# Sparse attention and maxout layer on one core: k, q and x of batches 1 to 3 transposed by DMA

## The chip, the cores and the metric

The kernel runs on one core of a Trainium2 chip. What counts is the device time of one execution in microseconds (us). The kernel before was run twice: 197.19 and 196.74 us, median 196.97.

## What is computed

Four batches, eight heads, 768 tokens, 64 values a head. Each token attends to the tokens less than 16 away, and to 24 summaries, one for each block of 32 tokens: of k the maximum, of v the mean. The result goes, token by token with its heads side by side, through a maxout layer.

```python
k_sum = k.reshape(B, H, nb, block, D).max(axis=3)
v_sum = v.reshape(B, H, nb, block, D).mean(axis=3)
scores_l = scale * np.matmul(q, k.transpose(0, 1, 3, 2))
mask_l = np.abs(pos[:, None] - pos[None, :]) < window
scores_s = scale * np.einsum('bhsd,bhnd->bhsn', q, k_sum) + np.log(block)
scores_all = np.concatenate([np.where(mask_l, scores_l, -1e9), scores_s], axis=-1)
a = softmax(scores_all)
x = np.matmul(a, np.concatenate([v, v_sum], axis=2))     # then (3072, 512)
out = np.maximum(x @ w1, x @ w2) @ w_out
```

## The kernel before

**Attention** goes by batch `b` (0 to 3), head pair `hp` (0 to 3) and group `grp` (0 to 2, 256 tokens each). For every batch and head pair, `prep` does this for k and for q:

- The load (L280) brings 384 KB into `kqf`, one of six buffers. Each partition gets six tokens that follow one another in a head, so a row of memory is 6 x 64 floats, 1,536 B.
- A cast (L359) writes bf16 into `kqb`, one of four buffers, with the two heads of a token side by side.
- TensorE turns it (L378): six 128x128 transposes into one PSUM bank.
- For k, DVE copies the bank to `kx` in token order (L393). Then it takes the maximum over each block (L399, L403, L407), copies the keys for the odd windows (L414) and puts the summaries in place (L418).
- For q, ACT copies the bank to `qx` (L424), in two halves of 64 partitions, one for each head.

`scores` multiplies `kx` and `qx` (L450), takes the exponential on ACT (L462) and, for batches 1 to 3, multiplies with a mask of zeros and ones on DVE (L471, L477). For batch 0 the mask is added on TensorE (L439). `values` multiplies with `vx` (L496); DVE takes the reciprocal of the sums (L508) and scales the result into `xs` (L510). After every second head pair TensorE turns `xs` (L520) and DVE copies it to `xt` (L525), the input of the layer.

v is loaded into `vf` in rows of one token, 256 B (L318), cast into `vx` on POOL (L359), and its copies for the odd windows and its summaries are spread inside `vx`; in batches 1 to 3 by DMAs on SyncE (L304).

**Maxout** has one unit for each batch and group, twelve in all: four `hidden` steps of eight matmuls (L596) with a relu on ACT (L601), and two `out` steps (L610, L617), an ACT copy (L359) and a store (L628). It computes max(h1, h2) w_out as h1 w_out + relu(h2 - h1) w_out, with `w1o` = w1 w_out made once (L580).

**The order** is made when the kernel is built. `Plan.run` steps through a model of time: each operation has an engine, a duration in us and a priority, and an engine takes the first ready operation of its list. What comes out is one fixed order for each engine; on the chip every engine follows its own in order and waits where it must. For SyncE (SP) the planner books `ISSUE` = 0.55 us for each DMA, has at most `DEPTH` = 4 under way, and sends one after the other. All 92 DMAs of the kernel before are issued by SyncE.

Of the kernel before, what the change touches and what calls it, by code (L numbers as in the profile page):

```python
# [13 lines left out]
BF16 = mybir.dt.bfloat16  # L14
# [48 lines left out]
class Plan:  # L63
# [6 lines left out]
        self.tasks, self.port = [], 0.0  # L70

    def op(self, engine, us, fn, read=(), write=(), change=(), touch=(), behind=(), prio=0.0, label="",
           port=False):
        t = Task()
        t.port = port or engine == "POOL"
        t.engine, t.us, t.fn, t.label = engine, us, fn, label
        t.prio = (prio, len(self.tasks))
        t.new, t.behind = [*write, *change], behind
        t.deps = {w for b in (*read, *change) for w in b.writers}
        for b in t.new:  # L80
            b.writers.append(t)
        for b in (*read, *touch, *t.new):
            b.users.append(t)
        self.tasks.append(t)
        return t
# [16 lines left out]
    def run(self):  # L102
        waiting = {e: [] for e in self.LAG}
        for t in sorted(self.tasks, key=lambda t: t.prio):
            waiting[t.engine].append(t)
        busy = dict.fromkeys(self.LAG, 0.0)
        sent = [0.0] * self.DEPTH
        order, tick = [], 0
        while len(order) < len(self.tasks):
            now = tick * 0.02  # L110
            for e, queue in waiting.items():
                if busy[e] > now or (e == "SP" and sent[-self.DEPTH] > now):
                    continue
                t = next((t for t in queue if self.ready(t, now)), None)
                if t is None:
                    continue
                t.start = now
                if e == "SP":
                    busy[e] = now + self.ISSUE
                    t.done = max(sent[-1], now + 0.4) + t.us  # L120
                    sent.append(t.done)
                else:
                    busy[e] = t.done = now + t.us
                    if t.port:
                        self.port = t.done
                queue.remove(t)
                order.append(t)
            tick += 1
            assert now < 1000, [t.label for q in waiting.values() for t in q]
        for t in order:  # L130
            t.fn()
        return order
# [3 lines left out]
def kernel(  # L136
# [14 lines left out]
    nc = tc.nc  # L151
    B, H, S, D = 4, 8, 768, 64
# [6 lines left out]
    NM, J, VW = S // 128, S // 128, 66  # L159
    NEG = -29952.0  # L160
    plan = Plan()
    op = plan.op
# [4 lines left out]
    def tiles(name, n, shape, dt):  # L167
        return [const.tile(shape, dt, name=f"{name}{i}") for i in range(n)]
# [5 lines left out]
    def bank(buf, n=512, dt=F32):  # L174
        a = bank_tile[:, buf.slot]
        return (a if dt is F32 else a.bitcast(BF16))[:, 0:n]

    kqf = Ring(tiles("kqf", 6, [128, 2, J * D], F32))
    kqb = Ring(tiles("kqb", 4, [128, J, 2, D], BF16))
    kxr = Ring(tiles("kx", 4, [128, 2, NM, 128], BF16))  # L180
    qxr = Ring(tiles("qx", 4, [128, 2, S], BF16))
    pbr = Ring(tiles("pb", 12, [128, 4, 192], BF16))
    vfr = Ring(tiles("vf", 1, [128, H, NM, D], F32))
# [91 lines left out]
    kqin, kx, qx, xt = {}, {}, {}, {}  # L275

    def load_kq(b, hp, prio):
        for n, src in enumerate((k, q)):
            f = kqin[b, hp, n] = Buf(kqf)
            op("SP", 1.05, lambda f=f, src=src: nc.sync.dma_start(  # L280
                out=f.ap[:], in_=src[b, 2 * hp:2 * hp + 2].rearrange("h (p j) d -> p h (j d)", j=J)),
               write=[f], prio=prio, label=f"load {'kq'[n]}{b}{hp}")

# [71 lines left out]
    def copy(engine, n, aps, label, us=None, **kw):  # L355
# [4 lines left out]
             "POOL": nc.gpsimd.tensor_copy}[engine](out=o, in_=i)  # L360
        op(engine, us or 0.06 + n * RATE[engine], fn, label=label, **kw)

    def prep(b, hp, prio, k_on, q_on):
        kx[b, hp], qx[b, hp] = Buf(kxr), Buf(qxr)
        tag = f"{b}{hp}"
        pss = []
        for n, eng in enumerate((k_on, q_on)):
            f, src = kqin[b, hp, n], Buf(kqb)
            copy(eng, 768, lambda f=f, src=src: (
                src.ap[:].rearrange("p j h d -> p h j d"),  # L370
                f.ap[:].rearrange("p h (j d) -> p h j d", d=D)),
                 read=[f], write=[src], prio=prio, label=f"cast {'kq'[n]}{tag}")
            ps = Buf(banks, "kq")
            pss.append(ps)

            def turn(src=src, ps=ps):
                for j in range(J):
                    nc.tensor.transpose(out=bank(ps, S, BF16)[:, 128 * j:128 * j + 128],  # L378
                                        in_=src.ap[:, j].rearrange("p h d -> p (h d)"),
                                        identity=identity[:])  # L380

            op("PE", J * 0.056, turn, read=[src], write=[ps], prio=prio, label=f"turn {'kq'[n]}{tag}")
        kps, qps = pss

        def order(ps):
            return bank(ps, S, BF16).rearrange("p (j c) -> p c j", j=J)

        main, odd, ks = Buf(Ring([None])), Buf(Ring([None])), Buf(ksr)

        def even():  # L390
            return kx[b, hp].ap[:, 0].rearrange("p m c -> p (m c)")

        op("DVE", 0.96, lambda: nc.vector.tensor_copy(out=even(), in_=order(kps)),  # L393
           read=[kps], write=[kx[b, hp], main], prio=prio, label=f"place k{tag}")
        def fold(k):
            return half.ap[:, 0:nb * k].rearrange("p (n g) -> p n g", g=k)

        half, one, two = Buf(hfr), Buf(Ring([None])), Buf(Ring([None]))
        op("DVE", 0.28, lambda: (lambda e: nc.vector.tensor_tensor(  # L399
            out=fold(16), in0=e[:, :, 0:16], in1=e[:, :, 16:32], op=ALU.max))(  # L400
                even().rearrange("p (n g) -> p n g", g=block)),
           read=[main], write=[half, one], prio=prio, port=True, label=f"max k{tag}")
        op("DVE", 0.18, lambda: (lambda e: nc.vector.tensor_tensor(  # L403
            out=half.ap[:, 384:576].rearrange("p (n g) -> p n g", g=8), in0=e[:, :, 0:8], in1=e[:, :, 8:16],
            op=ALU.max))(fold(16)),
           read=[one], write=[half, two], prio=prio, port=True, label=f"max k{tag}")
        op("DVE", 0.27, lambda: nc.vector.tensor_reduce(  # L407
            out=ks.ap[:, 0:nb], in_=half.ap[:, 384:576].rearrange("p (n g) -> p n g", g=8), axis=AX.X,
            op=ALU.max),
           read=[two], touch=[half], write=[ks], prio=prio, port=True, label=f"max k{tag}")  # L410
        for us, at, n, to, frm in ((0.2, 64, 64, slice(0, NM), slice(0, NM)),
                                   (0.14, 0, 32, slice(0, NM - 1), slice(1, NM)),
                                   (0.1, 0, 32, slice(NM - 1, NM), slice(0, 1))):
            op("DVE", us, lambda at=at, n=n, to=to, frm=frm: nc.vector.tensor_copy(  # L414
                out=kx[b, hp].ap[:, 1, to, at:at + n], in_=kx[b, hp].ap[:, 0, frm, at:at + n]),
               read=[main], write=[kx[b, hp], odd], prio=prio, port=True, label=f"odd k{tag}")
        for e, at in ((0, 96), (1, 32)):
            op("DVE", 0.2, lambda e=e, at=at: nc.vector.tensor_copy(  # L418
                out=kx[b, hp].ap[:, e, :, at:at + 32],
                in_=ks.ap[:].rearrange("p (o n) -> p o n", o=1).to_broadcast([128, NM, 32])),  # L420
               read=[ks, odd], write=[kx[b, hp]], prio=prio, port=True, label=f"sums k{tag}")
        for a in range(2):
            r = slice(64 * a, 64 * a + 64)
            op("ACT", 0.8, lambda a=a, r=r: nc.scalar.copy(  # L424
                out=qx[b, hp].ap[r, a, :], in_=order(qps)[r]),
               read=[qps], write=[qx[b, hp]], prio=prio, label=f"place q{tag}")
# [59 lines left out]
    def values(b, hp, grp, pb, prio):  # L486
        ps, tag = Buf(banks, "av"), f"{b}{hp}{grp}"
# [17 lines left out]
        if hp == 0:  # L505
            xt[b, grp] = Buf(xtr)
        x, x_t = xs[b, grp], xt[b, grp]
        op("DVE", 0.18, lambda: nc.vector.reciprocal(out=inv.ap[:], in_=av()[:, :, :, D:D + 1]),  # L508
           read=[ps], write=[inv], prio=prio, label=f"inv {tag}")
        op("DVE", 0.42, lambda: nc.vector.tensor_tensor(  # L510
            out=x.ap[:, hp % 2], in0=av()[:, :, :, 0:D],
            in1=inv.ap[:].to_broadcast([128, 2, 2, D]), op=ALU.mult),
           read=[ps, inv], write=[x], prio=prio, label=f"x {tag}")
        if hp % 2 == 0:
            return
        xp = Buf(banks, "x")

        def turn():
# [7 lines left out]
            out=x_t.ap[:, hp - 1:hp + 1, :].rearrange("p h n -> p (h n)"),  # L526
            in_=bank(xp, 512, BF16)), read=[xp], write=[x_t], prio=prio, label=f"xt {tag}")
# [182 lines left out]
```

## Time and profile before

| | |
|---|---|
| median of the two runs | 196.97 us |
| the profiled execution | 197.19 us |
| its span in the profile | 195.5 us |
| TensorE busy | 169.6 us, 87% |
| DVE busy | 120.1 us, 61% |
| ACT busy | 115.9 us, 59% |
| DMA packets on SyncE's queue, share of 16 engines' span | 61.0% |
| SyncE waiting in front of stores (L628) for ACT | 71.3 us |

The span is the profiled stretch on the core; the time of the same execution is 1.7 us longer. TensorE's busy share is of matmuls whose ends are modelled, so a full TensorE isn't one at its peak. Busy shares are means over the whole span, and the stages differ: in the first 50 us TensorE is busy for 30.2 us, after 80 us all the time. The profile also shows the clock that TensorE was granted: full nearly everywhere, 0.50 between 28 and 40 us.

### The profile page before, as it was taken

What the parts mean: (1) busy time and instruction counts of PE and PEld (TensorE: products, weight loads), DVE (VectorE), ACT (ScalarE), POOL (GpSimd) and SP (SyncE); (2) the same over time, 40 slices, a digit from 0 to 9 for tenths busy, and PEclk for the clock granted to TensorE, in tenths of its full rate; (3) what the DMA queues carried; (4) which work ended last, traced back from release to release, by engine and by line L of the source; (5) the groups of instructions that cost most, each with busy time, mean ns of one, the idle gap of its engine ahead of it and who ended that gap; (6) DMA issues with size and microseconds to landing.
All of it is one profiled execution on the core that took longest, in us unless ns stands there. A gap on an engine that the chain in (4) does not pass through costs nothing.

```text
span 195.5 us, 4320 instructions
## 1 busy us (share of the span) xinstructions
PE 169.6 (87%) x1688; PEld 121.8 (62%) x1688; DVE 120.1 (61%) x377; ACT 115.9 (59%) x183; POOL 29.7 (15%) x44
## 2 busy tenths in 40 slices
PE   0278553699999979999999999999999999999991
PEld 0166443688856546776867858587786675665740
DVE  6529999999869496741998853459878640000000
ACT  8297692855893843432999947169875542443512
POOL 7820395423000041000500000000000000000000
PEclk9999975589999999999999999999999999999998
DMA  5999999999999979997598152032020110220203
GB/s 178 263 255 282 376 385 390 245 273 334 237 232 322 211 197 294 324 212 198 170 230 291 66 161 107 5 117 62 3 107 3 54 57 21 86 96 15 107 0 107
DMA packets 29972, 34.57 MB, mean 177 GB/s; under 512 B 7616, under 2 KB 25568, under 8 KB 29952
## 3 DMA queue, kind: packets, MB, share of 16 engines
q1 hardware_dynamic: 29952, 34.30, 61.0%
q8 instruction: 13, 0.21, 0.5%
q14 instruction: 7, 0.06, 0.1%
HBM read 25.17 MB, written 6.29 MB: 161 GB/s over the span
## 4 chain that ended last, share of the span: by engine, by line
PE 61%; DMA 2%; ACT 2%; DVE 1%; issue 0%; ACTq 0%
PE banks L617 19%; PE banks L596 18%; PE banks L610 10%; PE banks L496 4%; PE banks L450 3%; PE banks L378 3%; PE banks L520 2%; DMA vx<-vx 2%; PE banks L338 1%; ACT g L601 1%; ACT qx L424 1%; DVE kqb L359 0%; ACT o L359 0%; ACT pb L462 0%; DVE pb L471 0%
## 5 line engine op out<-in xcount | busy, mean ns | idle before, releaser
L596 PE MATMUL banks<-xt,wd 128*128 128x256 bf16 x384 | 47.5, 273 | 0.5 <-DVE xt L525 0.5
L617 PE MATMUL banks<-wo,g 128*128 128x512 bf16 x192 | 46.0, 379 | 0.0
L596 PEld LDWEIGHTS <-wd 128*128 128x128 bf16 x384 | 35.9, 98 | 5.5 <-issue 0.7
L601 ACT ACTIVATE g<-banks 128x512 bf16<-128x512 f32 x48 | 28.7, 597 | 15.1 <-PE banks L596 14.2
L462 ACT ACTIVATE pb<-banks 128x512 bf16<-128x512 f32 x48 | 26.9, 598 | 13.7 <-PE banks L450 13.5
L359 ACT COPY o<-banks 128x512 f32<-128x512 f32 x24 | 14.1, 587 | 30.8 <-PE banks L617 30.3
L617 PEld LDWEIGHTS <-g 128*128 128x128 bf16 x192 | 17.7, 98 | 18.2
L378 PE MATMUL banks<-identity,kqb 128*128 128x128 bf16 x192 | 17.2, 237 | 13.1 <-ACT kqb L359 8.4
L424 ACT COPY qx<-banks 64x768 bf16<-64x768 bf16 x32 | 25.3, 790 | 3.4 <-PE banks L378 2.9
L610 PE MATMUL banks<-w1o,xt 128*128 128x512 bf16 x96 | 23.6, 379 | 0.0
L378 PEld LDWEIGHTS <-kqb 128*128 128x128 bf16 x192 | 13.6, 106 | 15.5 <-ACT kqb L359 9.4
L450 PE MATMUL banks<-qx,kx 128*128 128x128 bf16 (+2 forms) x208 | 18.6, 228 | 4.3 <-DVE kx L418 4.1
L450 PEld LDWEIGHTS <-kx 128*128 128x128 bf16 x208 | 15.3, 105 | 9.3 <-DVE kx L418 5.3
L496 PE MATMUL banks<-vx,pb 128*128 128x65 bf16 x384 | 18.8, 196 | 1.2 <-DMA vx<-vx 1.2
L496 PEld LDWEIGHTS <-pb 128*128 128x128 bf16 x384 | 16.9, 100 | 4.7 <-issue 1.4
L359 ACT CAST kqb<-kqf 128x768 bf16<-128x768 f32 x16 | 13.1, 831 | 10.9 <-DMA kqf<-in_q_dram 8.8
L510 DVE TENSOR_TENSOR xs<-banks,inv 128x256 bf16<-128x256 f32 x48 | 18.9, 413 | 0.2
L393 DVE COPY kx<-banks 128x768 bf16<-128x768 bf16 x16 | 15.2, 948 | 2.5 <-PE banks L378 2.3
L508 DVE RECIPROCAL inv<-banks 128x4 f32<-128x4 f32 x48 | 8.3, 178 | 9.7 <-PE banks L496 9.1
L359 POOL CAST vx<-vf 128x1536 bf16<-128x1536 f32 x6 | 8.8, 1501 | 34.6 <-DMA vf<-in_v_dram 34.6
L343 DVE CAST vx<-banks 32x264 bf16<-32x264 f32 x16 | 6.9, 432 | 10.4 <-issue 5.3
L610 PEld LDWEIGHTS <-xt 128*128 128x128 bf16 x96 | 8.7, 98 | 7.2
(48 smaller groups left out, 174.9 us busy)
## 6 DMA issues: line engine op xcount, KB each, us to landing
kqf<-in_k_dram SPq DMA_DIRECT2D x16, 384.0 KB, 7.4
kqf<-in_q_dram SPq DMA_DIRECT2D x16, 384.0 KB, 7.1
out_dram<-o SPq DMA_DIRECT2D x20, 256.0 KB, 2.0
wf<-in_moe_w_dram SPq DMA_DIRECT2D x8, 512.0 KB, 8.1
wf<-in_moe_w_out_dram SPq DMA_DIRECT2D x4, 512.0 KB, 6.7
vf<-in_v_dram SPq DMA_DIRECT2D x2, 768.0 KB, 8.5
vx<-vx SPq DMA_DIRECT2D x9, 165.0 KB, 3.7
vx<-vx SPq DMA_DIRECT2D x3, 396.0 KB, 10.4
```

What stands on the lines that cost most here:

```text
L359: {"DVE": nc.vector.tensor_copy, "ACT": nc.scalar.copy, "POOL": nc.gpsimd.tensor_copy}[engine](out=o, in_=i)
L378: nc.tensor.transpose(out=bank(ps, S, BF16)[:, 128 * j:128 * j + 128], in_=src.ap[:, j].rearrange("p h d -> p (h d)"), identity=identity[:])
L393: op("DVE", 0.96, lambda: nc.vector.tensor_copy(out=even(), in_=order(kps)), read=[kps], write=[kx[b, hp], main], prio=prio, label=f"place ...
L424: op("ACT", 0.8, lambda a=a, r=r: nc.scalar.copy(out=qx[b, hp].ap[r, a, :], in_=order(qps)[r]), read=[qps], write=[qx[b, hp]], prio=prio, ...
L450: nc.tensor.matmul(out=o[:, :, n0:n1], lhsT=w, rhs=qx[b, hp].ap[:, :, c:c + n1 - n0], start=(mask_on != "PE"), stop=(mask_on != "PE" or (i ...
L462: op("ACT", 0.6, lambda: nc.scalar.activation(out=pv(), in_=bank(ps).rearrange("p (i w q) -> p i w q", w=2, q=64), func=ACT.Exp, scale=scale),
L496: nc.tensor.matmul(out=av()[:, u, a, :], lhsT=pb.ap[:, 2 * u + a, 64 * par:64 * par + 128], rhs=vx[b].ap[:, par, 2 * grp + u, 2 * hp + a, ...
L510: op("DVE", 0.42, lambda: nc.vector.tensor_tensor(out=x.ap[:, hp % 2], in0=av()[:, :, :, 0:D], in1=inv.ap[:].to_broadcast([128, 2, 2, D]), ...
L596: nc.tensor.matmul(out=bank(ps)[:, 256 * s:256 * s + 256], lhsT=wd[n].ap[:, c, 128 * s:128 * s + 128], rhs=x.ap[:, c, :], start=(c == 0), ...
L601: op("ACT", 0.6, lambda n=n, ps=ps: nc.scalar.activation(out=g.ap[:, 2 * n:2 * n + 2, :].rearrange("p f n -> p (f n)"), in_=bank(ps), func ...
L610: nc.tensor.matmul(out=bank(ps), lhsT=x.ap[:, c, sl], rhs=w1o[c].ap[:], start=(c == 0), stop=False)
L617: nc.tensor.matmul(out=bank(ps), lhsT=g.ap[:, f, sl], rhs=wo[f // 2].ap[:, f % 2, :], start=False, stop=(f == FC - 1))
```

## The change

It concerns batches 1 to 3; batch 0 stays as it was.

- k and q of these batches are loaded with one token to a row: partition p gets tokens p, 128 + p, 256 + p and so on, in 12 rows of 256 B.
- `flip` is a new step: a transposing DMA from SBUF to SBUF, issued by SyncE. For k it writes `kx` directly (128x768), for q a new tile `qt` (two buffers), for x it writes `xt` (128x512 for two head pairs).
- So the turns of k, q and x on TensorE (L378, L520), the copies of k and x on DVE (L393, L525) and that of q on ACT (L424) are left out for these batches. q goes from `qt` to `qx` by two copies on DVE.
- The planner books 1.2 us on SyncE and 0.7 us of transfer for a flip, and 1.75 us for a load in short rows.

```diff
     def op(self, engine, us, fn, read=(), write=(), change=(), touch=(), behind=(), prio=0.0, label="",
-           port=False):
+           port=False, issue=None):
         t = Task()
+        t.issue = issue or self.ISSUE
...
-                    busy[e] = now + self.ISSUE
+                    busy[e] = now + t.issue
                     t.done = max(sent[-1], now + 0.4) + t.us
...
+    qtr = Ring(tiles("qt", 2, [128, J, 128], BF16))
...
             f = kqin[b, hp, n] = Buf(kqf)
-            op("SP", 1.05, lambda f=f, src=src: nc.sync.dma_start(
+            op("SP", 1.75 if b else 1.05, lambda f=f, src=src: nc.sync.dma_start(
+                out=f.ap[:].rearrange("p h (j d) -> p (h j) d", d=D),
+                in_=src[b, 2 * hp:2 * hp + 2].rearrange("h (j p) d -> p (h j) d", j=J))
+               if b else nc.sync.dma_start(
                 out=f.ap[:], in_=src[b, 2 * hp:2 * hp + 2].rearrange("h (p j) d -> p h (j d)", j=J)),
...
+    def flip(src, to, write, prio, label):
+        def fn():
+            i, o = src.ap[:], to()
+            names = "p a b c -> p (a b c)" if len(i.shape) == 4 else "p a b c e -> p (a b c e)"
+            nc.sync.dma_start_transpose(out=o, in_=i.rearrange(names))
+        op("SP", 0.7, fn, read=[src], write=write, prio=prio, label=label, issue=1.2)
+
     def prep(b, hp, prio, k_on, q_on):
...
+            if b:
+                pss.append(src)
+                continue
             ps = Buf(banks, "kq")
...
-        op("DVE", 0.96, lambda: nc.vector.tensor_copy(out=even(), in_=order(kps)),
-           read=[kps], write=[kx[b, hp], main], prio=prio, label=f"place k{tag}")
+        if b:
+            flip(kps, lambda: kx[b, hp].ap[:, 0], [kx[b, hp], main], prio, f"flip k{tag}")
+        else:
+            op("DVE", 0.96, lambda: nc.vector.tensor_copy(out=even(), in_=order(kps)),
+               read=[kps], write=[kx[b, hp], main], prio=prio, label=f"place k{tag}")
...
+        if b:
+            qt = Buf(qtr)
+            flip(qps, lambda: qt.ap[:], [qt], prio, f"flip q{tag}")
         for a in range(2):
             r = slice(64 * a, 64 * a + 64)
+            if b:
+                op("DVE", 0.26, lambda a=a, r=r: nc.vector.tensor_copy(
+                    out=qx[b, hp].ap[r, a, :], in_=qt.ap[r].rearrange("p m c -> p (m c)")),
+                   read=[qt], write=[qx[b, hp]], prio=prio, port=True, label=f"place q{tag}")
+                continue
...
         if hp % 2 == 0:
+            return
+        if b:
+            flip(x, lambda: x_t.ap[:, hp - 1:hp + 1, :].rearrange("p h (u n) -> p (h u) n", u=2), [x_t], prio,
+                 f"flip x{tag}")
             return
         xp = Buf(banks, "x")
```

As durations and engines change, the planner makes a new order for every engine. SyncE's changed list holds 134 DMAs, in this sequence: loads of batch 0; twelve loads of weights, mixed with k, q and v of batch 1; the first flips of batch 1 with its spreads of v; then flips, stores of batch 0 and loads of batch 2 in turn; flips of x of batch 1, some of them behind the load and the spreads of v of batch 2. For batch 2 it is the same pattern: eight flips of k and q with stores of batch 1 and loads of batch 3 between them, then the flips of x, three of group 0 to 2 for the first two head pairs, two spreads of v of batch 3, and the flip of x for group 0. TensorE's changed list has, after the last values of batches 1 and 2, no step of an earlier batch's maxout left in front of the first unit of that batch.

## The prediction

> **What bounds the kernel now.** First the page's slices and its chain, to find the engine that sets the end; then the chain in order of time, to price that engine's work; then the stage windows, to see what runs at its limit beside it.
>
> ```profile
> PE   0278553699999979999999999999999999999991
> ...
> DMA  5999999999999979997598152032020110220203
> ...
> PE 61%; DMA 2%; ACT 2%; DVE 1%; issue 0%; ACTq 0%
> ```
>
> Each digit is a slice of 4.9 us. TensorE is full from 88 us (slice 19) to the end, and holds 61% of the chain. The DMA engines are full, with three small dips, from 5 to 108 us, and mostly idle from there. So there are two limits, one after the other, and the change adds to the second what it takes from the first.
>
> ```profile
> 93.19 1.75 PE banks L596 x16
> ...
> 111.09 0.45 PE banks L520 x8
> ...
> 129.54 0.67 PE banks L378 x12
> ...
> 165.21 3.49 PE banks L596 x32
> 168.71 1.73 PE banks L610 x8
> 170.43 3.45 PE banks L617 x16
> ...
> 191.31 0.58 ACT o L359
> ```
>
> Columns: start, length, work. One maxout unit (a batch and a group) is 3.49 + 1.73 + 3.45 = 8.67 us; a turn by TensorE costs 0.67/12 = 0.056 us for k and q and 0.45/8 = 0.056 us for x. The first unit of batch 1 starts at 93.19; 4.2 us lie between the start of the last copy out (191.31) and the end of the span.
>
> ```profile
> 38.00:40.00 2.00, 1.90 (x29) 1.75 (x27) 1.97 (x7) 1.95 (x3) 0.00 (x0) 0.50 1.11 218
> ...
> 96.00:98.00 2.00, 2.00 (x20) 1.49 (x18) 2.00 (x9) 1.98 (x4) 0.00 (x0) 1.00 0.72 149
> ...
> 102.00:104.00 2.00, 2.00 (x35) 1.65 (x34) 1.82 (x9) 1.96 (x4) 0.00 (x0) 1.00 1.06 384
> ```
>
> The last three figures are TensorE's clock, DMA share (a full queue reads 1.06 to 1.12) and GB/s. At 38 us v of batch 1 loads in rows of 256 B: 218 GB/s with full engines. At 102 us k and q of batch 3 load in rows of 1,536 B: 384 GB/s. At 96 us the spreads of vx run; between 96 and 102 us about 170 GB/s.
>
> [...]
>
> **The change part by part.**
>
> *TensorE.* Gone are 12 x 2 x 6 = 144 turns of k and q and 18 x 4 = 72 of x: 216 x 0.056 = 12.1 us, all in the stretch where TensorE is full. This is the gain if nothing else comes in its place.
>
> *ACT and DVE.*
>
> ```profile
> L424 ACT COPY qx<-banks 64x768 bf16<-64x768 bf16 x32 | 25.3, 790 | 3.4 <-PE banks L378 2.9
> L393 DVE COPY kx<-banks 128x768 bf16<-128x768 bf16 x16 | 15.2, 948 | 2.5 <-PE banks L378 2.3
> ...
> L525 DVE COPY xt<-banks 128x512 bf16<-128x512 bf16 x24 | 9.8, 420 | 4.5 <-PE banks L520 4.0
> ```
>
> ACT loses 24 x 0.790 = 19.0 us. DVE loses 12 x 0.948 + 18 x 0.420 = 18.9 us and gains 24 copies of q from SBUF; a copy of half their columns takes 0.257 us (L414), so 0.257 to 0.514 us each, I take 0.40: +9.6. Neither ended the chain after 88 us, and TensorE's work covers them, so I credit nothing. The new copies wait for a flip with later reciprocals behind them, and those free the banks of values: a late flip also holds the other head pairs' values back.
>
> *SyncE.* 42 transposing DMAs are added to 92. A plain issue takes about 0.45 us; no row shows a transposing one, and the planner books 1.2 us. Between the first flip and that of x (2, 0) SyncE issues 26 flips and 39 plain DMAs: 26 x 1.2 + 39 x 0.45 = 49 us in the 90 us or so that this stretch lasts. Covered by the transfers, unless an issue costs over 2.8 us. No gain is possible here.
>
> *The DMA engines.* A load of k or q is 393 KB: 1.02 us at 384 GB/s, 1.80 at 218. Over 24 loads, +18.7 us. A flip of k or q moves 197 KB, one of x 131 KB. [...]
>
> *What that does to the order.* In the changed order TensorE has the units of batch b-1 used up when it comes to batch b's: the values of batch 2 are followed by two sums and at once by unit (2, 0), which needs the last flip of x for group (2, 0). All queues are in order, so TensorE stands until it lands. Ahead of it on SyncE's queue lie, in DMA time: loads of batch 0, 8 x 1.02 + 7.2 for v; weights 12 x 1.34; together 31.5. Loads of k and q of batches 1, 2 and six of 3: 22 x 1.80 = 39.6. Three v: 3 x 7.2 = 21.6. Spreads, 0.95 MB a batch at 170 GB/s, twice, and the odd part of batch 3: 14.8. [...] Ten stores x 0.68 = 6.8. Sum 131.3 us.
>
> How near to that do they run? The same prices for the kernel before, up to v of batch 3 landing (issued 78.8, landed 92.5), give 24 x 1.02 + 28.8 + 16.1 + 9.2 + 3.4 = 82.0 us in 92.5 - 1.3 = 91.2: a pace of 0.90. So (2, 0) can start at 1.3 + 131.3/0.90 = 147.2 us. From there the rest is TensorE's: six units, 52.0; scores and values of batch 3, 4 x 0.68 + 12 x 0.243 = 5.6; the end, 4.2. Together 61.8, and **the span becomes 209 us**. The profiled execution took 197.19 for its span of 195.5, so +1.7: 210.7; the median of the runs is 0.2 lower. I say **210 us**.
>
> Does TensorE arrive earlier? The same count up to the flip of (1, 0) gives 92.2 us, so 1.3 + 92.2/0.90 = 103.7 for unit (1, 0) in place of 93.19; from there three units, attention 2 and its sums are 26.0 + 5.6 + 1.35 = 33.0: TensorE is ready at 136.7, and stands some 10 us twice.
>
> **The rivals.**
>
> *TensorE stays the bound* (faster). Span 195.5 - 12.1 = 183.4, so 185 us. For it: 61% of the chain, and after 110 us the DMA engines are mostly idle. Against: (2, 0) would have to start by 121.6, with 131.3 us of transfers ahead. [...] It ends faster than before from the point where (2, 0) starts before 195.5 - 61.8 = 133.7: at a pace of 0.90 that is 119 us of transfers, which leaves flips 4.9 us, too little for 4.5 MB; at a pace of 1.0, flips of 246 GB/s do. So this case needs gapless transfers.
>
> *Flips are dear.* [...] At 170 GB/s flips cost 26 us instead of 17: + 10 us, 221. [...] A cycle makes it worse: kqb is freed by a flip, the cast needs kqb, the load needs the cast's buffer, and the flip stands behind loads in the same queue.
>
> *The words say more than the diff.* Masks on VectorE (L471) and odd values by DMA (L304) are in the kernel before already; no time comes from them.
>
> *The clock falls.* At 30 to 40 us, where TensorE idled, the granted clock was 0.50. If two stops of 10 us bring that back for a few us each, some 3 us a stop; inside the range.
>
> **How the numbers follow.** [...] Dear flips or the cycle: 0.28, 216 and up. TensorE-bound or nearly: 0.17, 185 to 193. A difference of 2% (3.9 us) is about what can be told from no change: faster means below 193.0, slower above 200.9. Of the likeliest case 0.14 falls between these. So faster 0.17, same 0.14, slower 0.69. The range, 191 to 230, leaves out most of the TensorE-bound end and the worst of the dear flips.
>
> **What would show it.** Right: the DMA digits stay at 9 to about 145 us; unit (2, 0) starts near 147 with TensorE idle before it, released by a flip of xt; L378 falls to 48 instructions and L424 to 8; k and q loads run near 218 GB/s. Wrong: TensorE full from 90 us on (rival one), flips of over 1 us of DMA time each (rival two), or SyncE busy issuing flips with idle DMA engines, where I have called the issue covered.

## The result, and the profile after

| | before | after |
|---|---|---|
| median of two runs | 196.97 us | 217.41 us |
| the profiled execution | 197.19 us | 217.56 us |
| its span | 195.5 us | 215.8 us |
| TensorE busy | 169.6 us, 87% | 167.4 us, 78% |
| TensorE's granted clock, mean | 0.961 | 0.913 |
| DMA packets on SyncE's queue, share | 61.0% | 83.1% |
| DMA packets under 512 B | 7,616 | 73,472 |

The ratio after to before is 1.104, interval 1.0975 to 1.1101: slower by a tenth. In the experiments below a time is the median of all runs of a kernel, while its ratio leaves out runs more than 1.5% above that kernel's fastest, so the two can differ by about 1%. The page of the changed kernel, slices first (5.4 us each), then the chain by engine:

```profile
PE   1292855999978699280896999947939999999992
...
PEclk9999795699999999757699699996997999999999
DMA  5999999999998999999999999976978244202202
...
PE 42%; DMA 19%; SPq 15%; DVE 14%; issue 5%; ACT 3%; POOL 0%; ACTq 0%; DVEq 0%
```

The full stretch of the DMA engines, which ended at 108 us before, now reaches the end of slice 26, 140 us, and is followed by a 7 and a 6. TensorE has holes beside it, at 87 to 92 and 97 to 103 us (slices 17 and 19) and at 143 to 147 us (slices 27 and 28). TensorE's share of the chain falls from 61 to 42%. What takes its place is DMA (2% before), SyncE's own instructions (SPq, not listed before) and DVE (1% before).

TensorE's timeline, the stops of over 3 us after 90 us; the brackets hold the idle time ahead and what ended it:

```profile
91.97 1.48 PE L343 MATMUL banks<-vx,ones 128*128 128x264 bf16 x6 [4.51 <-POOL vx L364]
...
103.17 5.11 PE L627 MATMUL banks<-xt,wd 128*128 128x256 bf16 x30 [6.66 <-DMA xt<-xs]
...
147.19 5.10 PE L627 MATMUL banks<-xt,wd 128*128 128x256 bf16 x30 [4.22 <-DMA xt<-xs]
...
160.09 0.61 PE L477 MATMUL banks<-qx,kx 128*128 128x128 bf16 x8 [3.48 <-DVE qx L447]
```

The first line is the sums of v of batch 2, released by the cast of that v. The second and third are units (1, 0) and (2, 0), both released by a flip of x. They resume at 103.17 and 147.19 us; 103.7 and 147.2 were forecast. The last stop was not forecast: the scores of batch 3 wait for a late flip of q and its copy on DVE.

What released (2, 0), from the chain in order of time:

```profile
140.94 0.78 SPq L372
...
142.43 2.01 SPq L309
...
144.53 2.62 DMA xt<-xs
...
147.19 5.12 PE banks L627 x30
```

L372 is a flip, L309 a spread of v. The x that is turned here was ready at 140.9 (a DVE instruction that starts at 140.51 and takes 0.42); SyncE got past the two spreads ahead of it at 144.5 only, and the flip then took 2.62 us from issue to landing. So the last link is SyncE's time, not a full DMA queue (the slices there read 7 and 6).

Stage windows at 76 us (k and q in rows of 256 B) and behind the stop of (2, 0); the last three figures are clock, DMA share and GB/s:

```profile
76.00:78.00 2.00, 2.00 (x42) 1.91 (x39) 1.88 (x9) 1.57 (x3) 0.00 (x0) 1.00 1.33 223
...
148.00:150.00 2.00, 2.00 (x12) 1.39 (x11) 0.00 (x0) 0.60 (x1) 0.00 (x0) 0.50 0.67 148
```

The short rows run at 223 GB/s, near the 218 that v showed before (38 to 40 us). After the stop of 4.2 us the granted clock is 0.50.

### The profile page after: what moved, and what is told of

Same layout as the page of the kernel before. It is cut to its first block, busy times and chain, and to the rows that moved or that the text cites. A ratio compares the mean times of both kernels' runs of the same rounds, so it can differ in the third digit from the quotient of the medians.

```text
span 215.8 us, 3917 instructions
## 1 busy us (share of the span) xinstructions
PE 167.4 (78%) x1472; PEld 115.0 (53%) x1472; DVE 105.5 (49%) x371; ACT 98.2 (45%) x159; POOL 29.2 (14%) x44
## 2 busy tenths in 40 slices
DMA packets 89683, 41.63 MB, mean 193 GB/s; under 512 B 73472, under 2 KB 85280, under 8 KB 89664
## 3 DMA queue, kind: packets, MB, share of 16 engines
q1 hardware_dynamic: 89664, 41.38, 83.1%
## 4 chain that ended last, share of the span: by engine, by line
PE 42%; DMA 19%; SPq 15%; DVE 14%; issue 5%; ACT 3%; POOL 0%; ACTq 0%; DVEq 0%
PE banks L627 15%; PE banks L648 11%; SPq L282 7%; DMA xt<-xs 5%; PE banks L641 5%; SPq L372 4%; DMA qt<-kqb 4%; PE banks L523 4%; DMA kqf<-in_q_dram 3%; PE banks L477 3%; PE banks L611 3%; DMA wf<-in_moe_w_dram 3%; DMA kx<-kqb 2%; SPq L309 2%; DVE kx L437 2%
## 5 line engine op out<-in xcount | busy, mean ns | idle before, releaser
L627 PE MATMUL banks<-xt,wd 128*128 128x256 bf16 x384 | 53.4, 296 | 10.9 <-DMA xt<-xs 10.9
L627 PEld LDWEIGHTS <-wd 128*128 128x128 bf16 x384 | 39.5, 106 | 20.2 <-issue 11.6
L537 DVE TENSOR_TENSOR xs<-banks,inv 128x256 bf16<-128x256 f32 x48 | 19.3, 417 | 14.4 <-DMA xt<-xs 14.0
L523 PE MATMUL banks<-vx,pb 128*128 128x65 bf16 x384 | 20.8, 204 | 6.1 <-DVE pb L498 2.4
L523 PEld LDWEIGHTS <-pb 128*128 128x128 bf16 x384 | 18.5, 105 | 10.6 <-issue 4.3
L364 DVE CAST kqb<-kqf 128x768 bf16<-128x768 f32 x13 | 7.2, 564 | 25.0 <-DMA kx<-kqb 16.4
L393 PE MATMUL banks<-identity,kqb 128*128 128x128 bf16 x48 | 5.7, 285 | 11.0 <-ACT kqb L364 6.5
L343 PE MATMUL banks<-vx,ones 128*128 128x264 bf16 x48 | 8.6, 332 | 4.5 <-POOL vx L364 4.5
L573 POOL TENSOR_TENSOR wd<-wf,wf 128x1024 bf16<-128x1024 f32 x4 | 9.7, 2430 | 10.4 <-DVE xs L537 6.1
L393 PEld LDWEIGHTS <-kqb 128*128 128x128 bf16 x48 | 4.4, 131 | 11.8 <-ACT kqb L364 7.1
```

What stands on the lines that cost most here:

```text
L364: {"DVE": nc.vector.tensor_copy, "ACT": nc.scalar.copy, "POOL": nc.gpsimd.tensor_copy}[engine](out=o, in_=i)
L523: nc.tensor.matmul(out=av()[:, u, a, :], lhsT=pb.ap[:, 2 * u + a, 64 * par:64 * par + 128], rhs=vx[b].ap[:, par, 2 * grp + u, 2 * hp + a, ...
L537: op("DVE", 0.42, lambda: nc.vector.tensor_tensor(out=x.ap[:, hp % 2], in0=av()[:, :, :, 0:D], in1=inv.ap[:].to_broadcast([128, 2, 2, D]), ...
L573: op(wd_on, 2.1 if wd_on == "POOL" else 1.2, lambda: (nc.gpsimd if wd_on == "POOL" else nc.vector).tensor_tensor(out=wd[n].ap[:], in0=fs[1 ...
L627: nc.tensor.matmul(out=bank(ps)[:, 256 * s:256 * s + 256], lhsT=wd[n].ap[:, c, 128 * s:128 * s + 128], rhs=x.ap[:, c, :], start=(c == 0), ...
```

## The experiments

Two theories stand at the start. *Theory 1*, the prediction's: the volume of transfers ahead of the flips of x sets units (1, 0) and (2, 0). *Theory 2*: SyncE, which stands before stores and issues everything in order, sets them. *Theory 3* came up with the trace: the way of x itself (values, `xs`, issue and landing of a flip) leaves TensorE with nothing to do for 4 to 5 us at the end of batch 1 and of batch 2.

Each ratio is to the kernel before, run beside it on the same chip (its medians there: 195.5 to 196.3 us).

### Stores issued by ACT

```diff
-                nc.sync.dma_start(out=out[b * S + at:b * S + at + n, :], in_=o.ap[0:n])
+                nc.scalar.dma_start(out=out[b * S + at:b * S + at + n, :], in_=o.ap[0:n])
```

> The changed kernel with its 28 stores issued by ACT, right behind ACT's own copies, in place of SyncE; SyncE's order is else the same. Theory 1 (volume: the DMA engines' pace sets when unit (2, 0) can start): the volume is the same, so (2, 0) starts no earlier than 143 us (147.2 in the changed kernel), and the time is 213 to 219 us. Theory 2 (SyncE in order: flips stand behind stores that wait 36 us in all for ACT's copies): these waits go, (1, 0) starts 6 to 8 us earlier than 103, (2, 0) at 132 to 138, and the time is 201 to 208 us.

220.03 us, ratio 1.127 (1.120 to 1.133), 1 us above theory 1's numbers. SyncE's share of the chain falls from 15 to 5%. Unit (1, 0) resumes at 101.93 us, 1.2 us earlier, and unit (2, 0) does not move. TensorE's and SyncE's timeline of this kernel:

```profile
147.24 6.16 PE L627 MATMUL banks<-xt,wd 128*128 128x256 bf16 x30 [5.32 <-DMA xt<-xs]
```

```profile
79.86 7.37 SPq L282 DMA_DIRECT2D kqf<-in_k_dram  x1
...
140.08 1.18 SPq L309 DMA_DIRECT2D vx<-vx  x2
144.60 3.96 SPq L372 DMA_TRANSPOSE xt<-xs  x3
```

That (2, 0) stays where it was is not a clean result. SyncE is past the two spreads at 141.3, 3.2 us earlier than in the changed kernel, but issues the flip for (2, 0), the first of the three, at 144.60 only; in the changed kernel it follows the spreads at once (past them at 144.45, issued at 144.53). What takes the 3.3 us isn't shown. Without them (2, 0) would have come at about 143.9 (an estimate, 147.24 less 3.3), which is still 6 us behind the latest that theory 2 allowed. So waiting in front of stores explains at most some 3 us of (2, 0), and theory 2's numbers fall in this form.

The first line of the second fence shows something else that holds SyncE: the DMA right behind a load of v takes it 7.37 us although the trace names no wait for it. The changed kernel has the same behind its loads of v: a load of k at 42.03 us with 8.29, one at 125.25 with 7.45. What keeps SyncE there isn't shown.

### Rows of 1,536 B with the flips kept

```diff
-            op("SP", 1.75 if b else 1.05, lambda f=f, src=src: nc.sync.dma_start(
-                out=f.ap[:].rearrange("p h (j d) -> p (h j) d", d=D),
-                in_=src[b, 2 * hp:2 * hp + 2].rearrange("h (j p) d -> p (h j) d", j=J))
-               if b else nc.sync.dma_start(
+            op("SP", 1.75 if b else 1.05, lambda f=f, src=src: nc.sync.dma_start(
```

> The changed kernel with k and q of batches 1 to 3 loaded in rows of 1,536 B again, the planner's figures and so all orders unchanged. The flips then put the tokens in another order, so this leaves out the right order of tokens in kx and qx; the work is the same. Theory 1 (volume): 22 loads up to (2, 0) cost 0.78 us less each, 17 us of transfers, 19 us at the pace of 0.90; (2, 0) would start at the time when TensorE is ready, 134 to 138, and the time is 200 to 208 us. Theory 2 (SyncE in order, and its issue of 1.25 us a flip): little changes, 212 to 217 us.

205.48 us, ratio 1.041 (1.032 to 1.049). This kernel leaves out the right order of tokens in `kx` and `qx`; the order of all instructions is that of the changed kernel. Unit (2, 0) comes 12.4 us earlier:

```profile
134.79 4.76 PE L624 MATMUL banks<-xt,wd 128*128 128x256 bf16 x30 [3.76 <-DMA xt<-xs]
```

Theory 1's 134 to 138 and its time hold, and the rows alone are worth 0.063 of the time before. By volume, the 22 short-row loads ahead of that unit would give 22 x 0.78/0.90 = 19.1 us; two thirds of it are seen, so the rest of the way there isn't volume alone.

### The short rows alone, in the kernel before

Only the load is changed, and the copies take the turned tile as it comes, since it is in token order then.

```diff
+                out=f.ap[:].rearrange("p h (j d) -> p (h j) d", d=D),
+                in_=src[b, 2 * hp:2 * hp + 2].rearrange("h (j p) d -> p (h j) d", j=J))
+               if b else nc.sync.dma_start(
...
+            if b:
+                return bank(ps, S, BF16)
```

> The kernel before with one part of the change alone: k and q of batches 1 to 3 loaded in rows of 256 B (turned on TensorE and placed in token order as before; the planner's figures unchanged). Theory 1 (volume): 114.3 us of transfers ahead of (2, 0) at a pace of 0.90 are done at 128, just when TensorE wants it (130.2), and 84.2 ahead of (1, 0) at 95, 2 us late: 197 to 199 us. Theory 2: no SyncE waits are added, 196.5 to 198. A third: short rows alone are most of the loss (they hold up the head pairs one after the other): over 205 us.

205.69 us, ratio 1.048 (1.042 to 1.054). Theory 1's number missed, and so did theory 2's; what was listed third, over 205 us, is what came. TensorE's timeline, before and with short rows, at the end of its wait for the last spread of vx of batch 1:

```profile
72.38 0.49 PE L496 MATMUL banks<-vx,pb 128*128 128x65 bf16 x11 [0.72 <-DMA vx<-vx]
```

```profile
79.38 0.49 PE L501 MATMUL banks<-vx,pb 128*128 128x65 bf16 x11 [0.60 <-DMA vx<-vx]
```

The stretch ahead of 88 us, which the prediction read as "the DMA engines are full" and left at that, ended on a transfer already. Twelve of the short-row loads (eight of batch 1, four of batch 2) are issued ahead of this spread: 12 x 0.78/0.90 = 10.4 us more by volume. The wait ends 7.0 us later than before, and the median grew by 9.9 us over that of the kernel before on the same chip, so the size is right and no more.

### Flips of k and q alone, in short and in long rows

x is turned on TensorE again:

```diff
-        if b:
+        if False:
             flip(x, lambda: x_t.ap[:, hp - 1:hp + 1, :].rearrange("p h (u n) -> p (h u) n", u=2), [x_t], prio,
```

> The changed kernel with x of all batches turned on TensorE again; k and q keep their short rows and flips. Theory 1 (volume): 126.3 us of transfers ahead of (2, 0), so it starts at 141 to 143, and the time is 204 to 209 us. Theory 3 (of the loss, a fixed part is the way of x: values, xs, issue and landing of a flip, 4 to 5 us in which TensorE has nothing else, at the end of batch 1 and of batch 2): both stops at the first unit of a batch go, and the time falls by 8 us or more below what volume alone gives, to 200 or less.

208.21 us, ratio 1.068 (1.057 to 1.078): theory 1's number, and theory 3's falls. But not by theory 1's way. It had (2, 0) wait for volume until 141 to 143; the trace has it at 137.94, with no stop in front of it. TensorE stands elsewhere, before the scores of batches 2 and 3, for DVE's copy of a flipped q:

```profile
107.77 1.01 PE L477 MATMUL banks<-qx,kx 128*128 128x128 bf16 x8 [3.91 <-DVE qx L447]
...
137.94 3.66 PE L627 MATMUL banks<-xt,wd 128*128 128x256 bf16 x32
...
145.65 0.61 PE L477 MATMUL banks<-qx,kx 128*128 128x128 bf16 x8 [3.19 <-DVE qx L447]
```

The second kernel has the long rows of above as well, and so leaves out the order of tokens too:

> As the run with x on TensorE, and k and q of batches 1 to 3 loaded in rows of 1,536 B (this leaves out the right order of tokens in kx and qx; the work is the same). 109 us of transfers ahead of (2, 0). Theory 1 (volume): they are done at 122, before TensorE wants them, TensorE is the bound without the 8.0 us of turns of k and q: 188 to 192 us. Theory 2 (issue and order on SyncE hold up the flips of k and q whatever the volume): TensorE stops before the scores of each batch as it does with short rows, 198 us or more.

193.77 us, ratio 0.987 (0.979 to 0.994): just above theory 1's span of numbers, far from the rival's. Without short rows, the flips of k and q pay, though little: the 144 turns they take off TensorE are worth 144 x 0.056 = 8.1 us, and 2.6 are seen. The stop that the rival named is there once, before the scores of batch 2, whatever the rows:

```profile
97.30 1.01 PE L474 MATMUL banks<-qx,kx 128*128 128x128 bf16 x8 [4.47 <-DVE qx L444]
```

### Flips of x alone, in the kernel before

`flip` and its planner costs are added to the kernel before, and only x uses it.

```diff
+        if b:
+            flip(x, lambda: x_t.ap[:, hp - 1:hp + 1, :].rearrange("p h (u n) -> p (h u) n", u=2), [x_t], prio,
+                 f"flip x{tag}")
+            return
```

> The kernel before with the flips of x alone (batches 1 to 3); k and q as before the change. Theory 1 (volume): nine us more of transfers, most of them after 90 us, where there is room, and 4.05 us less on TensorE: 193 to 195 us. Theory 3 (the way of x costs 4 to 5 us at each batch where TensorE has nothing else): 2 such stops less the 4 us saved, 199 to 203 us.

199.38 us, ratio 1.017 (1.011 to 1.024). Theory 1's gain is not there, theory 3's loss is, at the low end. Of the two stops that theory 3 named only one came: 3.49 us before (1, 0), which resumes at 96.95. The chain of this kernel, in order of time, has two flips of batch 1 on it:

```profile
75.86 8.71 DMA xt<-xs
...
91.90 5.01 DMA xt<-xs
```

A flip of 131 KB takes 8.71 us to land; six loads of 393 KB are issued in the 9 us ahead of it (67.08 to 71.83 us). The 18 flips of x are 8.1 us of transfers at the 0.45 us measured below.

### What a flip costs: spare flips, spare copies

In the kernel with k and q alone, 18 flips are added where x is turned; they read a constant and write a tile that is no longer used, and nothing waits for them.

```diff
+            if b:
+                at = (6 * b + 2 * grp + hp // 2) % 8 * 512
+                nc.sync.dma_start_transpose(
+                    out=w1t.ap[:, at:at + 512].rearrange("p (a c) -> p a c", a=4),
+                    in_=ones[:, 0:4].rearrange("p a c -> p (a c)"))
```

> The run with x on TensorE (short rows, flips of k and q), and 18 spare flips of 128x512 added where TensorE's turns of x stand in the program: a constant tile is transposed into a tile that is no longer read. They have the transfers and SyncE's issue of the flips of x, but wait for nothing, and nothing waits for them. Theory 1 (volume and issue): most of the 9.2 us that lie between x on TensorE (208.2) and the changed kernel (217.4) come back: 213 to 217 us. Theory 3 (the way of x: values, xs, issue, landing, first unit): the spare flips cost little, 208 to 211 us.

224.70 us, ratio 1.151 (1.147 to 1.155); the span is 16.3 us over that of the kernel without them (222.6 and 206.3), 0.91 us for each flip, more than either theory allowed. Their transfers, 18 x 0.45 us as measured below, are 8.1 us, half of that. So a plain copy of the same size in the same places was next:

```diff
-                nc.sync.dma_start_transpose(
-                    out=w1t.ap[:, at:at + 512].rearrange("p (a c) -> p a c", a=4),
+                nc.sync.dma_start(
+                    out=w1t.ap[:, at:at + 512],
```

> The run with spare flips, each of the 18 made a plain copy of the same 131 KB from SBUF to SBUF at the same place in SyncE's order (issue 0.4 to 0.6 us in place of 1.25 us; the bytes are the same). With spare flips the span was 16.3 us over the run without any (206.3). Theory 1a (the bytes of a flip are the cost): 219 to 226 us again. Theory 1b (SyncE's issue of 1.25 us is the cost, one behind the other, not covered by transfers): 18 x 0.5 us in place of 18 x 1.25, at most 9 us over 208.2: 210 to 217 us.

216.07 us, ratio 1.103 (1.098 to 1.108), as theory 1b had it; 7.5 us over, 0.42 for each. SyncE's timeline of the two kernels, at the first flip of k of batch 2 (99.09 us without spares), with six spares ahead of it from 89.8 us on:

```profile
89.77 3.95 SPq L552 DMA_TRANSPOSE w1t<-ones  x3
...
106.41 1.22 SPq L372 DMA_TRANSPOSE kx<-kqb  x1
```

```profile
89.76 1.85 SPq L552 DMA_DIRECT2D w1t<-ones  x3
...
101.98 1.28 SPq L372 DMA_TRANSPOSE kx<-kqb  x1
```

The flip of k comes 7.3 us later with six spare flips and 2.9 later with six copies. Of this, 1.1 and 0.3 us were there already at the load ahead of the first spare (issued at 87.32 without spares, 88.39 and 87.62 with them). That leaves 6.2 us, 1.04 for each flip, and 2.6, 0.43 for each copy. This is near their issue, 1.22 to 1.28 us and 0.59 us, and the flips are well above their transfer: on an otherwise idle queue, late in the changed kernel, a flip of x keeps the engines busy for some 0.45 us (290 GB/s). SyncE's time is on the path here. The split is bounded, not measured: of the 8.8 us between the two kernels some 2 may be transfer (an estimate: a copy of 131 KB at the 384 GB/s of the long rows is 0.34 us, against 0.45 for a flip, and 18 x 0.11 = 2.0).

### Flips for some batches only

All conditions of the change become `b >= 2`, `b >= 3`, or `b >= 3` with x of all batches on TensorE:

```diff
-        if b:
+        if b >= 3:
```

> Short rows and flips for batches 2 and 3, batch 1 as before the change. Theory 1 (volume): 116 us of transfers ahead of (2, 0), done at 130, about when TensorE wants it; but short rows of batch 2 lie ahead of the spreads of v of batch 1, at which TensorE stood in the kernel before already (72.4 us): 2 to 5 us there. TensorE loses 8.1 us of turns: 191 to 196 us. Theory 3 (the way of x): a stop of 4 to 5 us at the first unit of batch 2 on top, 196 to 201 us.

> Loads in short rows and flips for batch 3 alone; batches 1 and 2 as before the change. Theory 1 (volume): [...]TensorE stays the bound and loses 48 turns of k and q and 24 of x, 72 x 0.056 = 4.0 us: 193 us. Theory 2 (SyncE in order): the eight flips of batch 3 stand behind stores and each other, TensorE stops before the scores of batch 3 for 3 to 8 us, and the time is 197 to 201 us.

> Short rows and flips of k and q for batch 3 alone, x of all batches on TensorE. In batch 3 the DMA engines have room and three units of batch 2 still stand ahead when its x comes. Theory 1 (volume): flips of x are free there, and without them TensorE has 24 turns more, 1.3 us: 194 to 195 us, against 193.1 with them. Theory 3 (the way of x costs wherever it is): without them it is faster, 190 to 192 us.

| flips for | us | ratio, interval |
|---|---|---|
| batches 2 and 3 | 202.55 | 1.032 (1.024 to 1.041) |
| batch 3 | 193.14 | 0.978 (0.972 to 0.984) |
| batch 3, k and q alone | 193.43 | 0.989 (0.985 to 0.994) |

In the kernel before, the DMA digits from 107.5 us on are 5 and less. What the change adds for batch 3 is 14.4 us of transfers, an estimate: eight loads x 0.78, and eight flips of 197 KB and six of 131 KB at the 290 GB/s measured above (0.68 and 0.45 us). With batch 3 alone the change gains, against both kernels: its interval is clear of 1, though not of the 2% set as the measure of a difference, and for k and q alone the gain is below that. The slices of the page of batch 3 (4.8 us each, an execution of 194.02 us):

```profile
PE   0276565889469989999989999999999999999991
...
DMA  5999999999999979989998619996037221120203
```

TensorE has no hole after 100 us. The flips of k and q are issued at 113 to 128 us, while TensorE has attention and maxout of batches 1 and 2 to do, and those of x at 141 to 152, where the digits of the DMA engines are 7 and less. The gain is that of the turns: 48 + 24 of them at 0.056 us are 4.0 us, and 2.2% of 195.8 is 4.3. k and q alone: 2.7 us worked out, 1.1% or 2.1 us measured. So theory 1 holds for batch 3 (193 forecast; for k and q alone 194 to 195, missed by 0.6), theory 2 falls, and the flips of x do not cost there what theory 3 said: without them the time is no shorter. With batch 2 as well, both theories' numbers were too low; its trace shows a dozen small stops (the longest 2.36 and 2.21 us, for masks and copies on DVE), and which part of the change makes them wasn't separated.

### Long rows, put in order by engines

To keep the long rows and the right token order, k goes from its flipped tile to `kx` on DVE, and q to `qx` on ACT, both with the strided read that the copies from PSUM had; x is on TensorE.

```diff
+            kt = Buf(qtr)
+            flip(kps, lambda: kt.ap[:], [kt], prio, f"flip k{tag}")
+            op("DVE", 0.9, lambda: nc.vector.tensor_copy(
+                out=even(), in_=kt.ap[:].rearrange("p j c -> p c j")),
...
+                op("ACT", 0.8, lambda a=a, r=r: nc.scalar.copy(
+                    out=qx[b, hp].ap[r, a, :], in_=qt.ap[r].rearrange("p j c -> p c j")),
```

> Flips of k and q for batches 1 to 3 with rows of 1,536 B, the tokens put in order afterwards: DVE copies a flipped k into kx with a stride of six tokens, ACT a flipped q into qx as it did before; x on TensorE. Three qt buffers in place of two and eleven pb in place of twelve. 109 us of transfers ahead of (2, 0), TensorE without the 8.0 us of turns. Theory 1 (volume): 190 to 195 us, as with unordered tokens (193.8); DVE and ACT, 12 and 19 us busier, are covered. Theory 2 (the longer way of k and q stops TensorE before the scores): 198 us or more.

211.49 us, ratio 1.085 (1.080 to 1.090). Theory 1 missed; theory 2's "198 us or more" holds. From this kernel's costliest groups:

```profile
L448 ACT COPY qx<-qt 64x768 bf16<-64x768 bf16 x24 | 36.5, 1521 | 2.4 <-DMA qt<-kqb 2.0
```

The copy that took 790 ns from PSUM takes 1,521 from SBUF with the same strided read. From 120 to 140 us ACT is busy for 9.88 of every 10 us and TensorE for 7.5 to 8.0, so ACT is the bound there; what bounds the other stretches wasn't separated. Put in order this way, the long rows bring no gain.

## Why the prediction was right, point by point

**The bound.** Right in kind: the two units waited for flips late in SyncE's queue, and came within 0.6 us of the forecast. Volume is the larger part of it: long rows in the same order moved the second by 12.4 us. The sums were better than their parts, though. The 131.3 us hold 17.0 for 26 flips, which was my assumption; the trace of the kernel before shows no flip. At the 290 GB/s that flips of x show in the changed kernel, their 4.46 MB take 15.4 us, and (2, 0) comes at 145.4 in place of 147.2 (an estimate). (2, 0) was released by SyncE's issue and a 2.62 us landing, and in the variants the same count is off by more: 1.3 + (131.3 - 22 x 0.78)/0.90 = 128.1 against 134.79 with long rows, 141 to 143 against 137.94 with x on TensorE. The agreement to 0.1 us is largely chance.

**TensorE, "216 x 0.056 = 12.1 us".** Right as a count, but not "all in the stretch where TensorE is full". In the kernel before, the 48 turns of k and q of batch 1 stand between 37 and 66 us, ahead of TensorE's last stop at 72 us; by the digits TensorE is full from slice 16 (73 us), not slice 19. So at most 168 x 0.056 = 9.4 us were to be had there. L378 with 192 turns became 48:

```profile
L627 PE MATMUL banks<-xt,wd 128*128 128x256 bf16 x384 | 53.4, 296 | 10.9 <-DMA xt<-xs 10.9
...
L393 PE MATMUL banks<-identity,kqb 128*128 128x128 bf16 x48 | 5.7, 285 | 11.0 <-ACT kqb L364 6.5
```

Half of the 12.1 was paid back within TensorE's busy time: the hidden matmuls took 273 ns before and 296 now, at a mean clock of 0.961 and 0.913; 5.9 us over 384 of them.

**ACT and DVE credited with nothing.** Nothing speaks against it: in the experiment with only k and q in long rows all three engines are relieved and the whole gain is 2.6 us, less than TensorE's turns alone would give. The new copies took 0.35 us each (0.40 estimated). Where TensorE waited for them, three times, it stood 5.0 us in all, 3.5 of them at 160 us.

**SyncE's issue, "Covered by the transfers".** This step failed. The issue itself was right (1.2 booked, 1.22 to 1.28 measured), but the cover is not there: in the kernel with k and q alone, spare flips cost 0.91 us each and spare copies 0.42. Averaging 49 us of issue over a 90 us stretch hid that SyncE stands for 7 to 8 us behind the loads of v of batches 1 to 3 (8.29, 8.17 and 7.45 us; in the second, 7.6 are a store's wait for ACT) and then has to issue flips one after another.

**The DMA engines.** Short rows, +18.7 us of DMA time: with the order kept, they cost 0.063 to 0.081 of the time before (the changed kernel against the long-row one; k and q alone, short against long), 12 to 16 us. Their price was taken from v, whose loads the trace counts in packets of 1,024 B (425 packets and 0.44 MB from 38 to 40 us), while the new loads of k and q go in packets of 256 B; that both ran near 220 GB/s is what made it fit. So the 218 GB/s that the prediction gave for rows of 256 B are of packets of 1,024 B; the 223 of the changed kernel are the figure for packets of 256 B (1,694 of them with 0.43 MB, 76 to 78 us). What the flips of x cost by the same table of four is 0.036 to 0.054, 7 to 11 us, while their turns should have given 72 x 0.056 = 4.0 back. Their transfers are 18 x 0.45 = 8.1 us; what the count left out, by the spare flips, is the issue. These two comparisons include a new order by the planner, so their size holds only roughly. Step by step the loss is: flips of k and q with long rows -0.013, short rows +0.081, flips of x +0.036, together the 0.104.

**The two stops, "some 10 us twice".** Half right. The first was 4.51 + 6.66 = 11.2 us, in two pieces; the first piece was a wait for v of batch 2, only the second one for x. The second stop was 4.2: TensorE came to it at 142.97 in place of 136.7, with 2.8 us of small stops and two stretches at a clock near half (102 to 107 and 120 to 124 us) behind it. That didn't move the unit, since the flip set it.

**The rest, "Together 61.8".** It was 215.8 - 147.19 = 68.6, and this 6.8 is the whole of the miss in the span (209 against 215.8). 3.5 are the stop before the scores of batch 3; some 1.8 the first steps of (2, 0), 5.10 us where 30 such matmuls took 3.49 x 30/32 = 3.3 before; about 1 the half clock at 162 to 164 us. The remainder is not traced. The rival of the clock had named "some 3 us a stop"; 1.8 came at the second, and 5.9 us on the hidden matmuls of the whole kernel.

**The rivals.** TensorE as the bound is what happens when only batch 3 is changed: 0.978. The case that came, paced by the DMA engines, had a weight of 0.55. Dear flips fell as a price of the transfer (0.45 us for one of x), but a flip's issue, 1.22 to 1.28 us, is a cost of that kind that I had ruled out.

## What to carry to other kernels

Before work goes to a DMA queue, count what lies ahead of its first consumer in the order of issue, with the row size of each load and the issue time of each DMA; engines that are "mostly idle" later in the kernel (digits of 5 and less from 107.5 us on before the change) didn't help there. Don't count issue time as covered from an average: here the issuer stood 7 to 8 us behind loads of v, and each flip added afterwards cost 0.91 us. The same change, made only for the last batch, behind which the queue runs dry (digits of 3 and less from 149 us on), kept its gain: 0.978.

## What the runs showed of the hardware

- A transposing DMA took SyncE 1.22 us for 128x512 and 1.28 for 128x768 bf16 (medians of the changed kernel); a plain copy of 131 KB took 0.59 (the kernel with spare copies, 97.98 to 101.28 us).
- On an otherwise idle queue a transposing DMA of 131 KB kept the DMA engines busy for some 0.45 us, about 290 GB/s (the changed kernel, 179 to 184 us).
- The load of k after a 1.57 MB load of v took SyncE 8.29 us (at 42.03) and 7.45 (at 125.25) in the changed kernel, and 7.37 (at 79.86) in the one with stores on ACT, with no wait named.
- Loads of k and q in rows of 256 B ran at 223 GB/s (76 to 78 us), in rows of 1,536 B at 384 (the kernel before, 102 to 104 us).
- After the stop of 4.2 us the granted clock in the changed kernel was 0.50 from 148 to 151 us, and it was 0.50 again from 162 to 164 us, after a stop of 3.5.
- ACT's copy of 64x768 bf16 took 790 ns from PSUM (the kernel before) and 1,521 from SBUF (long rows put in order), with the same strided read.
